# Transposes of keys, queries and outputs moved from TensorE to VectorE by 32-blocks, in a fused DeltaNet and maxout-FFN kernel

## The chip, the cores and the metric

The kernel runs on one core of a Trainium2 chip. The metric is the time on the device in microseconds (us), as the median of a few executions; lower is better. Every run named here was of the undisturbed ("fast") state, and every kernel gave correct results.

The engines are TensorE (PE in the profile, with its weight loads as PEld), VectorE (DVE), ScalarE (ACT), GpSimd (POOL) and SyncE (SP). SyncE only issues transfers. "SPq", "ACTq" and "POOLq" stand for transfers issued by that engine. Each engine works through its own instructions in order: in one run below VectorE stands idle for 43.5 us before six instructions whose data have not landed yet.

## What is computed

A recurrent attention over four batches, eight heads, 768 tokens and a head size of 48, followed by a feed-forward part (FFN) with a maximum over three products:

```python
for t in range(S):                                     # attention, all of (B=4, H=8), D=48
    y[:, :, t] = q_t @ state
    v_old = state.T @ k_t                              # k_t normalised
    state = state + beta_t * outer(k_t, v_t - v_old)
x = y.transpose(0, 2, 1, 3).reshape(B * S, H * D)      # 3072 x 384
h = maximum(maximum(x @ w1, x @ w2), x @ w3)           # 384 -> 768
return h @ w_out                                       # 768 -> 384
```

The kernel cuts the sequence into 12 chunks of 64 tokens. A chunk has two *units* (two batches each), so there are 24 units. Two chunks make a *group* with 512 rows for the FFN. While the FFN of group m runs in 22 pieces, the attention of group m+1 is slipped between its pieces, units of group m+2 are prepared, and data for later ones is loaded.

## The kernel before: the parts that matter

A unit's keys and queries have to be turned before their products (the *gram*, `p_g`) can be made. TensorE does it with eight transposes, and ScalarE copies the result out of PSUM:

```python
def turn(n, parts=(0, 1)):
    kqt = kqts[n]                        # work.tile([128, NP, 2, 2, C], name="kqt", bufs=6)
    p_t = ps_two("p_t")
    for i in parts:                      # keys, queries
        src = (kpad[n % NK], qpad[n % NQ])[i]
        for j in range(NP):              # NP = 4 pairs of heads
            nc.tensor.transpose(p_t[:, i, j * 128 : (j + 1) * 128],
                                src[:, 2 * j : 2 * j + 2], ident)
    ...
    nc.scalar.copy(kqt..., p_t...)
```

A chunk's attention output `y` becomes the input `xt` of the FFN in the same way:

```python
def to_x(c):
    ...
    for g in range(2):
        for t in range(KT):              # KT = 3
            nc.tensor.transpose(p_x[:, g, t * 128 : (t + 1) * 128],
                                y_f[:, g, t * 128 : (t + 1) * 128], ident)
    ...
    copied(c, xt, p_x...)                # ScalarE
```

Which step of the attention comes after which piece of the FFN stands in a table (k, q: products with the state; t: turn; g: gram; z, j, u, s: solve and state; y: output; x: to_x; the digit is the chunk or unit in the group):

```python
LINKS = {
    0: "k0 q0", 1: "t0 t1", 2: "g0 g1", 3: "z0 z1 t2", 5: "j0 j1", 6: "t3",
    7: "u0 g2", 9: "s0 g3", 11: "k1 q1", 13: "u1 y0", 15: "s1", 16: "x0",
    18: "y1", 20: "x1",
}
...
for m in range(1, GROUPS):               # not under manual_schedule
    for i, _ in enumerate(ffn(m)):
        ... loads of k, q, v; solve of group m + 2 from piece 12 on, on VectorE
        links(m + 1, LINKS.get(i, ""))
```

The first part of the kernel keeps its program order by `manual_schedule`. In the loop above there is none, so the order of the instructions on each engine is settled when the kernel is built.

## Time and profile before

| | before |
|---|---|
| time, median of 3 | 612.01 us (610.31 to 614.21) |
| TensorE busy | 560.7 us, 92% |
| VectorE busy | 315.0 us, 52% |
| bytes moved | 45.38 MB |
| from the start of one group's FFN to the next, groups 1 to 4 | 87.4, 87.4, 86.1, 76.5 us |

Three lines of the page of the kernel before: a group of instructions has its line in the kernel's file (L339), engine, operation, output and inputs, shapes, count, then busy time and mean duration in ns, then the idle time just before them. The first line is a queue with packets, megabytes and its share of sixteen DMA engines.

```profile
q1 hardware_dynamic: 132640, 34.01, 29.2%
...
L339 ACT COPY kqt<-p_t 128x512 f32<-128x512 f32 (+1 forms) x32 | 25.0, 796 | 22.2 <-PE p_t L333 22.2
...
L333 PE MATMUL p_t<-ident,kpad 128*128 128x128 f32 x96 | 16.1, 295 | 7.0 <-DVE pt L365 4.7
```

The turning costs TensorE instructions and ScalarE a copy for each unit. What TensorE waited for between 207 and 545 us, that is in groups 1 to 4 (waiting instruction, releaser, total, times, longest):

```profile
PE p_o L721 <- DVE h L707: 2.4, 3, 1.0
PE p_h L697 <- DVE h L707: 0.7, 2, 0.3
```

That is all: 3.1 us in 337.5. The kernel before has almost no slack on TensorE and almost no waits to remove.

### The profile page before, as it was taken

How to read it: one execution, taken by the hardware profiler on the slowest of the kernel's cores; microseconds unless marked ns; L12 is line 12 of the kernel's file. 1: busy time of each engine (PE TensorE's matmuls, PEld its weight loads, DVE VectorE, ACT ScalarE, POOL GpSimd, SP SyncE). 2: the span in 40 equal slices, each digit the busy share in tenths (PEclk: the TensorE clock that was granted, in tenths of full speed). 3: DMA queues.
4: the chain of work that ended last, by engine and by line, in shares of the span. 5: the costliest groups of instructions: out<-in, count | busy, mean ns of one | idle time of the engine just before them, and what ended most of it. 6: DMA issues, size and time to landing. Idle time of an engine off the chain costs nothing.

```text
span 611.2 us, 18549 instructions
## 1 busy us (share of the span) xinstructions
PE 560.7 (92%) x8270; PEld 345.4 (57%) x8270; DVE 315.0 (52%) x730; ACT 155.1 (25%) x284; POOL 70.7 (12%) x102
## 2 busy tenths in 40 slices
PE   5547884998999999999999999999999999999997
PEld 5436774787655565555655545655556545554443
DVE  3454789859369652389532498522696322101110
ACT  4222444643322232221332211331112111110000
POOL 6331544432001000010000000000000000000000
PEclk9755578999999999999999999999999999999999
DMA  9964892942641363321542321522104000010002
GB/s 154 176 168 109 186 194 94 236 96 61 115 67 27 87 117 61 72 54 26 105 85 60 66 48 27 109 54 62 19 15 92 18 2 3 14 40 0 0 1 52
DMA packets 142095, 45.38 MB, mean 74 GB/s; under 512 B 127680, under 2 KB 137728, under 8 KB 142016
## 3 DMA queue, kind: packets, MB, share of 16 engines
q1 hardware_dynamic: 132640, 34.01, 29.2%
q10 hardware_dynamic: 8576, 8.26, 4.8%
q0 software_dynamic: 800, 1.93, 1.2%
q8 instruction: 65, 1.06, 0.7%
q14 instruction: 14, 0.11, 0.1%
HBM read 29.98 MB, written 14.16 MB: 72 GB/s over the span
## 4 chain that ended last, share of the span: by engine, by line
PE 71%; DVE 15%; DMA 6%; issue 3%; SPq 2%; ACT 1%; POOL 1%; POOLq 0%; ACTq 0%; DVEq 0%
PE p_h L697 39%; PE p_o L721 16%; DMA w_bits<-in_moe_w_dram 3%; DVE y_bl L452 3%; DVE tmp L448 3%; PE p_g L355 3%; PE p_t L333 3%; PE p_k L584 2%; PE p_u L612 2%; PE p_y L650 2%; PE p_q L584 1%; DVE h L707 1%; PE p_j L566 1%; PE p_e L515 1%; DVE t L499 1%
## 5 line engine op out<-in xcount | busy, mean ns | idle before, releaser
L697 PE MATMUL p_h<-xt,w_sb 128*128 128x512 f32 (+1 forms) x702 | 297.9, 571 | 1.8 <-DVE xt L683 1.2
L697 PEld LDWEIGHTS p_h<-xt,w_sb 128*128 128x128 f32 x702 | 129.9, 193 | 124.4 <-issue 114.8
L707 DVE TENSOR_TENSOR h<-h,p_h 128x512 f32<-128x512 f32 (+1 forms) x78 | 50.2, 644 | 135.1 <-PE p_h L697 134.9
L721 PE MATMUL p_o<-wo_sb,h 128*128 128x384 f32 x288 | 96.9, 490 | 2.4 <-DVE h L707 2.4
L721 PEld LDWEIGHTS p_o<-wo_sb,h 128*128 128x128 f32 x288 | 53.4, 190 | 40.8 <-DVE h L707 6.8
L452 DVE TENSOR_TENSOR y_bl<-y_bl,tmp 128x31 f32<-128x31 f32 (+20 forms) x154 | 54.0, 351 | 4.1
L448 DVE TENSOR_TENSOR tmp<-x_bl,y_bl 128x31 f32<-128x31 f32 (+20 forms) x154 | 52.8, 343 | 4.2
L705 ACT COPY h<-p_h 128x512 f32<-128x512 f32 (+1 forms) x39 | 21.5, 551 | 119.0 <-PE p_h L697 118.9
L274 POOL TENSOR_TENSOR v_t<-v_t,nrm 128x768 f32<-128x768 f32 x12 | 17.9, 1492 | 275.8 <-DMA v_t<-in_v_dram 179.8
L355 PE MATMUL p_g<-kqt 64*64 64x64 f32 (+1 forms) x1280 | 32.1, 248 | 3.9 <-ACT kqt L339 3.8
L355 PEld LDWEIGHTS p_g<-kqt 64*64 64x64 f32 x1280 | 27.7, 147 | 9.6 <-ACT kqt L339 5.7
L729 ACT COPY o_sb<-p_o 128x384 f32<-128x384 f32 x24 | 11.4, 477 | 79.5 <-PE p_o L721 78.3
L339 ACT COPY kqt<-p_t 128x512 f32<-128x512 f32 (+1 forms) x32 | 25.0, 796 | 22.2 <-PE p_t L333 22.2
L499 DVE STREAM_TRANSPOSE t<-ut 32x256 f32<-32x256 f32 x48 | 20.7, 432 | 6.0 <-DMA ut<-y_d 5.2
L612 PEld LDWEIGHTS p_u<-v_t,ut 64*64 64x64 f32 x768 | 14.4, 148 | 15.6 <-issue 8.5
L612 PE MATMUL p_u<-v_t,ut 64*64 64x48 f32 x768 | 16.1, 234 | 7.3 <-DVE ut L569 4.5
L333 PE MATMUL p_t<-ident,kpad 128*128 128x128 f32 x96 | 16.1, 295 | 7.0 <-DVE pt L365 4.7
L333 PE MATMUL p_t<-ident,qpad 128*128 128x128 f32 x96 | 16.7, 301 | 6.1 <-DMA qpad<-in_q_dram 5.7
L235 POOL TENSOR_TENSOR w_sb<-mant,up 128x384 int32<-128x384 int32 x18 | 18.1, 1005 | 26.9 <-DVE mant L231 18.1
L365 DVE TENSOR_TENSOR pt<-p_g,mask 128x512 f32<-128x512 f32 x24 | 16.5, 690 | 8.7 <-PE p_g L355 8.5
L208 ACT ACTIVATE mant<-w_bits 128x384 f32<-128x384 f32 x24 | 13.3, 556 | 22.3 <-DMA w_bits<-in_moe_w_dram 11.8
L373 ACT COPY at<-p_g 128x512 f32<-128x512 f32 x20 | 11.6, 585 | 29.0 <-DVE pt L365 26.5
(95 smaller groups left out, 489.7 us busy)
## 6 DMA issues: line engine op xcount, KB each, us to landing
w_bits<-in_moe_w_dram ACTq DMA_DIRECT2D x14, 384.0 KB, 4.2
at_d<-at SPq DMA_DIRECT2D x36, 128.0 KB, 2.5
qpad<-in_q_dram SPq DMA_DIRECT2D x48, 96.0 KB, 3.2
v_t<-in_v_dram SPq DMA_DIRECT2D x24, 192.0 KB, 4.0
out_dram<-o_sb SPq DMA_DIRECT2D x48, 96.0 KB, 2.2
kpad<-in_k_dram SPq DMA_DIRECT2D x44, 96.0 KB, 3.9
y_d<-y_bl SPq DMA_DIRECT2D x12, 256.0 KB, 3.3
ut<-y_d SPq DMA_DIRECT2D x48, 64.0 KB, 2.8
```

The lines of the kernel that those rows point to most:

```text
L333: nc.tensor.transpose(p_t[:, i, j * 128 : (j + 1) * 128], src[:, 2 * j : 2 * j + 2], ident,)
L339: nc.scalar.copy(kqt.rearrange("p j b i t -> p i (j b) t")[:, some], p_t.rearrange("p i (x t) -> p i x t", t=C)[:, some],)
L355: nc.tensor.matmul(p_g[rows(bb ^ (g * i)), par, c0 : c0 + C * (1 + whole)], kq[:, 0], kq if whole else kq[:, i],)
L448: nc.vector.tensor_tensor(out=t_v, in0=row.to_broadcast(t_v.shape), in1=column.to_broadcast(t_v.shape), op=ALU.mult,)
L452: nc.vector.tensor_tensor(out=rest, in0=rest, in1=t_v, op=ALU.subtract)
L499: nc.vector.transpose(out=t1[c % NU][block(bb ^ g), g], in_=ut[c % NU][block(bb), g, :, 0:BL])
L584: nc.tensor.matmul(p_b[rows(bb), par, c0 : c0 + D], kqt[g][rows(par), j, bb ^ g, i], st[rows(par), bb ^ g, g, j],)
L612: nc.tensor.matmul(p_v[rows(bb ^ g), g, h], ut[c % NU][rows(bb), g, h], rhs[rows(bb), g, h],)
L697: nc.tensor.matmul(p_h, w_sb[i][:, t, f * 128 : (f + 1) * 128], xt[:, t, lo : lo + w], start=(t == 0), stop=(t == KT - 1),)
L705: nc.scalar.copy(h, p_h)
L707: nc.vector.tensor_tensor(out=h, in0=h, in1=p_h, op=ALU.max)
L721: nc.tensor.matmul(p_o, hs[f][:, i * 128 : (i + 1) * 128], wo_sb[:, f], start=(f == 0), stop=(f == FT - 1),)
```

## The change

The intent is to take the transposes off TensorE. VectorE can turn 32x32 blocks, so the transfers have to put the right blocks in the right partitions.

- Units 12 to 23: `load_blocks` brings keys (on SyncE) and queries (on GpSimd) in 16 transfers a unit, and `turn_blocks` turns them with four VectorE instructions. The tail of each buffer is set to zero by GpSimd.
- Chunks 4 to 11: `y_blocks` writes the output to DRAM in two transfers and reads it back in four, all on SyncE; `turn_y` turns it with one VectorE instruction. The FFN weights are loaded with rows ordered "(p t)" to fit.
- The buffers of both kinds, `turned` and `y_q`, share the four of tag `w_bits`.
- The table of links is rearranged.

```diff
+    def load_blocks(n):
+        c, g = divmod(n, 2)
+        for i in range(2):
+            t = turned[n, i] = work.tile(
+                [128, 2, TURNED], FP32, name="turned", tag="w_bits", bufs=4
+            )
+            nc.gpsimd.memset(t[:, :, TURNED - 48 : TURNED], 0.0)
+            for bb in range(2):
+                for par in range(2):
+                    for db in range(2):
+                        ...
+                        (nc.sync, nc.gpsimd)[i].dma_start(out=t[p0 : p0 + 32, ...], in_=(k, q)[i][...])
+    def turn_blocks(n):
+        kqts[n] = work.tile([128, NP, 2, 2, C], FP32, name="kqt", bufs=6)
+        for i in range(2):
+            t = turned.pop((n, i))
+            for bb in range(2):
+                nc.vector.transpose(out=kqts[n][:, :, bb ^ (n % 2), i]..., in_=t[:, bb, ...])
 ...
+    def y_blocks(c):
+        y = yts.pop(c)
+        y_d = dram.tile([32, 2, 4, DM], FP32, name="y_x")
+        for g in range(2):
+            nc.sync.dma_start(out=y_d[:, g]..., in_=y[:, g]...)
+        y_q = yqs[c] = work.tile([128, 8, 96], FP32, name="y_q", tag="w_bits", bufs=4)
+        for a in range(4):
+            nc.sync.dma_start(out=y_q[32 * a : 32 * (a + 1)], in_=y_d[:, :, :, 96 * a : 96 * (a + 1)]...)
+    def turn_y(c):
+        ...
+        nc.vector.transpose(out=xts[m][:, :, cc * 256 : (cc + 1) * 256]..., in_=yqs.pop(c)...)
 ...
     LINKS = {
-        0: "k0 q0", 1: "t0 t1", 2: "g0 g1", 3: "z0 z1 t2", 5: "j0 j1", 6: "t3",
-        7: "u0 g2", 9: "s0 g3", 11: "k1 q1", 13: "u1 y0", 15: "s1", 16: "x0",
-        18: "y1", 20: "x1",
+        0: "k0 q0", 1: "t0 t1", 2: "g0 g1", 3: "z0 z1", 4: "t2", 5: "j0 j1",
+        6: "u0 t3", 7: "g2", 8: "s0", 9: "g3", 10: "k1 q1", 12: "u1 y0", 13: "x0",
+        14: "s1", 16: "y1", 17: "x1 X0", 21: "X1",
     }
```

(Cut: the access patterns; the same index change in gram and the products with the state; strided reads in `to_x`; the places where loads are issued. In the new table "x" sends a chunk's output to DRAM and back, "X" turns it.)

More of the change, by code (lines that the diff above doesn't have):

```diff
@@ L105, in rows, with dims @@
         return slice(C * bb, C * (bb + 1))
+    def dims(par):
+        return slice(DP * par, DP * par + D)
     def load(src, dst, n, queues):
@@ L172 @@
         for w_t, w in zip(w_sb, (moe_w1, moe_w2, moe_w3)):
-            bits = w.bitcast(U32).rearrange("(t p) f -> p t f", p=128)
+            bits = w.bitcast(U32).rearrange("(p t) f -> p t f", p=128)
             cols = slice(f * 128, (f + 1) * 128)
@@ L342, in turn @@
         )
+    BLOCKS = 12
+    TURNED = 32 + NP * 2 * D + 16
+    turned = {}
+    def load_blocks(n):
[8 more added lines that the diff above has]
+                    for db in range(2):
+                        p0, at = DP * par + 32 * db, 32 * (1 - db)
+                        (nc.sync, nc.gpsimd)[i].dma_start(
+                            out=t[p0 : p0 + 32, bb, at : at + NP * 2 * D].rearrange(
+                                "p (j x) -> p j x", j=NP
+                            ),
+                            in_=(k, q)[i][
+                                2 * bb + g, :, c * C : (c + 1) * C, :
+                            ].rearrange(
+                                "(j two) (r tb) d -> two r j (tb d)", two=2, tb=2
+                            )[par],
+                        )
+    def turn_blocks(n):
[3 more added lines that the diff above has]
+            for bb in range(2):
+                nc.vector.transpose(
+                    out=kqts[n][:, :, bb ^ (n % 2), i].rearrange(
+                        "p j (r tb) -> p j tb r", tb=2
+                    ),
+                    in_=t[:, bb, 32 : 32 + NP * 2 * D].rearrange(
+                        "p (j tb d) -> p j tb d", tb=2, d=D
+                    )[:, :, :, 0:32],
+                )
     def gram(n, parts=(0, 1), queues=one_queue, copy=nc.scalar.copy):
@@ L351, in gram @@
                 for bb in range(2):
-                    kq = kqt[rows(par), j, bb ^ g]
+                    kq = kqt[dims(par), j, bb ^ g]
                     for i in (0,) if whole else parts:
@@ L585, in times_state @@
                             p_b[rows(bb), par, c0 : c0 + D],
-                            kqt[g][rows(par), j, bb ^ g, i],
-                            st[rows(par), bb ^ g, g, j],
+                            kqt[g][dims(par), j, bb ^ g, i],
+                            st[dims(par), bb ^ g, g, j],
                         )
@@ L668, in to_x @@
                     p_x[:, g, t * 128 : (t + 1) * 128],
-                    y_f[:, g, t * 128 : (t + 1) * 128],
+                    y_f[:, g, t::KT],
                     ident,
@@ L675, in to_x @@
         copied(c, xt, p_x[:, :, 0 : KT * 128].rearrange("p g (t x) -> p g t x", t=KT))
+    yqs = {}
+    def y_blocks(c):
+        y = yts.pop(c)
+        y_d = dram.tile([32, 2, 4, DM], FP32, name="y_x")
+        for g in range(2):
+            nc.sync.dma_start(
+                out=y_d[:, g].rearrange("t b x -> b t x"),
+                in_=y[:, g].rearrange("p h d -> p (h d)"),
+            )
+        y_q = yqs[c] = work.tile([128, 8, 96], FP32, name="y_q", tag="w_bits", bufs=4)
+        for a in range(4):
+            nc.sync.dma_start(
+                out=y_q[32 * a : 32 * (a + 1)],
+                in_=y_d[:, :, :, 96 * a : 96 * (a + 1)].rearrange(
+                    "t g b x -> t (g b) x"
+                ),
+            )
+    def turn_y(c):
+        m, cc = divmod(c, 2)
+        if m not in xts:
+            xts[m] = work.tile([128, KT, TOK], FP32, name="xt")
+        nc.vector.transpose(
+            out=xts[m][:, :, cc * 256 : (cc + 1) * 256].rearrange(
+                "p t (b x) -> p b t x", x=32
+            ),
+            in_=yqs.pop(c).rearrange("p b (x t) -> p b t x", t=KT),
+        )
     def copied(c, to, of):
@@ L850, in links @@
             f, i = name[0], int(name[1])
-            if f in BY_CHUNK and m < GROUPS:
+            if f in "xX" and 2 <= m:
+                if m < GROUPS:
+                    (y_blocks if f == "x" else turn_y)(2 * m + i)
+            elif f in BY_CHUNK and m < GROUPS:
                 BY_CHUNK[f](2 * m + i)
@@ L857, in links @@
             elif f in BY_UNIT and m + 1 < GROUPS:
-                BY_UNIT[f](4 * (m + 1) + i)
+                n = 4 * (m + 1) + i
+                (turn_blocks if f == "t" and n >= BLOCKS else BY_UNIT[f])(n)
     by_hand = ExitStack()
@@ L891 @@
             load_k(i - 15)
-            if i < 30:
-                load_q(i - 15)
+            if i < 29:
+                load_blocks(i - 15)
     some(solving, 40)
@@ L901 @@
                 load_k(n)
-                if n % 4 < 3:
-                    load_q(n)
+                if i < 20:
+                    load_blocks(n)
             if m + 2 < GROUPS:
                 n0 = 4 * (m + 2)
-                if i == 2:
-                    load_q(n0 + 3)
+                if i in (1, 3):
+                    load_blocks(n0 + 2 + i // 3)
                 if i in (6, 9):
```

## The prediction

> **What bounds the kernel now.** I read the page's first two parts, then the busy time by stage, the chain that ended last in order of time, the timelines of each engine in one stage, and who waited for whom.
>
> The page of the kernel before, busy time, slices and the chain by line:
> ```profile
> PE 560.7 (92%) x8270; PEld 345.4 (57%) x8270; DVE 315.0 (52%) x730; ACT 155.1 (25%) x284; POOL 70.7 (12%) x102
> ...
> PE   5547884998999999999999999999999999999997
> ...
> DVE  3454789859369652389532498522696322101110
> ```
> PE is at 9 tenths from about slice 9 on; VectorE comes next, and unevenly. The mean hides stages, so I cut the span where the feed-forward (FFN) of each group of four units begins. The busy time of each engine in five such stretches:
> ```profile
> 207.27:294.70 87.43, 86.06 (x1290) 49.49 (x1289) 51.46 (x124) 21.68 (x36) 3.04 (x2) 1.00 0.34 67
> 294.70:382.14 87.44, 86.04 (x1290) 49.46 (x1289) 50.77 (x120) 21.63 (x36) 2.95 (x2) 1.00 0.34 68
> 382.14:468.28 86.14, 85.83 (x1289) 49.61 (x1289) 46.77 (x106) 19.08 (x30) 1.47 (x1) 1.00 0.25 52
> 468.28:544.80 76.52, 76.52 (x1002) 41.63 (x1001) 19.00 (x29) 12.51 (x20) 0.00 (x0) 1.00 0.11 24
> 544.80:611.00 66.20, 61.83 (x156) 29.34 (x155) 8.25 (x12) 5.90 (x11) 0.00 (x0) 0.99 0.07 15
> ```
> The columns are length, busy time of PE, weight loads, VectorE, ScalarE and GpSimd, clock, DMA share, GB/s. In groups 1 to 4 PE is busy 98.4 to 100% of the time at full clock: what is taken off PE there shortens the kernel, until something else has to be waited for. The last stretch, with FFN alone, takes 61.8 us of PE time; the other 15 to 26 us of a group are the next group's attention, and the transposes are in those. The chain in order of time (start, length, what), one group's pieces of it:
> ```profile
> 302.06 1.75 PE p_t L333 x16
> ...
> 312.52 1.02 PE p_t L333 x8
> ...
> 322.71 0.87 PE p_t L333 x8
> ...
> 377.61 0.66 PE p_x L667 x6
> ```
> The chain runs through the transposes, so they are paid for in full.
>
> **What the Trainium skill says.** "VectorE: DVE Perf Modes", section "The three transpose paths": TensorE turns a whole 128x128 tile into PSUM, VectorE turns 32x32 blocks separately, SBUF to SBUF. That is why the change must have the right 32-blocks placed by DMA first. The trace times both kinds: 128x512 stream transposes take 690 ns and 32x256 ones 432 ns, so about 1.0 ns an element of a row plus 0.17 us, and a TensorE transpose in a row costs 1.75/16 = 0.109 us of the chain, though a single one is shown as 295 to 301 ns. "DMA: Bandwidth & Descriptors", section "Anatomy of one DMA": a transfer has a fixed cost of about 2 us, mostly the receipt. The trace agrees: 2.0 us for a 2 KB transfer, 2.2 to 4.0 us for the ordinary ones. "SBUF — State Buffer", section "Who interferes with whom": a VectorE instruction with two SBUF inputs blocks against a GpSimd instruction that reads SBUF, one with a single input outside the two-port modes does not. The trace agrees: an update of y_bl with 112 columns took 1.43 us instead of 0.28 while the scaling of v_t ran on GpSimd. The new block transposes have one input, so this should not touch them.
>
> **The change part by part.**
>
> *Off PE.* Units 12 to 23 are turned during groups 1 to 3, four in each. A unit has 8 transposes; a group 1.75 + 1.02 + 0.87 = 3.64 us, three groups 10.9 us. Chunks 4 to 11 are turned in groups 1 to 4, two in each, 6 transposes in 0.65 us: 8 x 0.65 = 5.2 us. Together 16.1 us, all on the chain. That is the most the intended saving can be: 612.0 - 16.1 = 595.9 us, or 2.6%. ScalarE also loses 12 copies of 1.0 us and 8 of 0.8 us, and the bank pairs in PSUM are less in demand; ScalarE was not the bound, so this is worth nothing by itself.
>
> *Onto VectorE.* A unit needs 4 block transposes of 128x256, each like the 256-element row above, 0.43 us: 1.7 us, 12 units 20.7 us. A chunk's output is one of 128x768: 0.17 + 768 x 1.0 ns = 0.95 us, 8 chunks 7.6 us. So 28 us, 8.8 us in a group that had 51 of 87 us: 60 of about 82, 73%. That fits in the mean. It isn't even, though: the block solve runs in the last third of a group, and there (256.0 to 294.7) VectorE is busy 31.8 of 38.7 us, from 263.7 on almost without a gap. The two output transposes fall right there.
>
> *Onto the queues.* A unit no longer loads q in two transfers with 192-byte rows, but has 16 transfers of 128 rows of 384 B, 8 for k on SyncE and 8 for q on GpSimd. k is still loaded untransposed as well. On the SyncE queue a transfer occupies about 0.55 us (8 loads of ut: 4.15 to 5.44 us). A group adds 32 and takes away 8, and the outputs add 2 x 6: 36 x 0.55 = 20 us more beside some 54 x 0.57 = 31 us, within 82 us. GpSimd gets 32 x 0.55 = 18 us, where it had 3. Bytes: 8 x 128 x 2 x 384 B = 0.79 MB a unit less 0.20 MB of q, so +2.4 MB a group, and the outputs out and back 2 x 0.79 = 1.6 MB: 5.9 to about 9.8 MB. At the 21.5 ns a packet of 256 B that queue 1 shows (29.2% of 16 x 611 us over 132,640 packets), so perhaps 30 ns at 384 B, that is 10 to 14 us of all sixteen engines' time more, share 0.34 to about 0.5. The transfers stay hidden in bulk.
>
> *New waits.* The output of a group's second chunk now takes a path through DRAM before the next group can begin: addition 0.95, write issue and landing 0.6 + 3.0, four reads 2.2 + 3.0, transpose 0.95, and hand-overs, about 12 us. Between the last y (after piece 16) and the next group PE has one FFN piece of 2.58 us and four of 3.87: 18 us. So it fits by 6 us, if neither the SyncE queue, in order, nor VectorE is held up. The blocks, y_q and the w_bits share four buffers; the second unit of the next group gets its buffers only when the two outputs have been turned.
>
> *The rearranged links.* Attention steps move up one or two pieces, filling the places of the transposes. A small effect of either sign: PE's idle time in groups 1 and 2 is only 1.4 us each.
>
> *The solve.* The gram of a group's last unit stays at piece 9 and starts the solve, so the solve begins about 3.6 us earlier in the group while the group is 5 us shorter. With 1.9 us of output transposes in its way it ends about 1.5 us after the next group begins (before: 293.8 against 294.7), and y_d and ut take some 9 to 12 us more (before: ut landed near 302). p_z, now about 14 us into the group, had 9 us of room and keeps 1 to 4.
>
> *Elsewhere.* Chunks 0 to 3 are transposed from rows with a stride of three: 24 weight loads, under 1 us if at all. Contracting over 48 instead of 64 rows doesn't change the columns streamed, so I count nothing.
>
> *Sum.* -16.1 us, plus 0 to 2 us at each of four group boundaries (output path), 0 to 2 us at three (solve and ut), and 0.3 to 0.5 us per group for maxima that come late behind block transposes: around 4 us given back. 612.0 - 16.1 + 4 = 600, and with the rearranged links, made to fill exactly these holes, I say 599.
>
> **The rivals.** (1) VectorE takes the bound in the last third of each group: the maxima of h queue behind solve and output transposes. For it: the only PE waits in groups 1 and 2 are already there, for h. Against it: one transpose is under 1 us, an FFN piece lasts 2.58 us and has two PSUM buffers. It would give back 2 to 3 us a group, for 604 to 608. (2) The path through DRAM or the late ut becomes the wait at group boundaries. For it: margins of 6 and of 1 to 4 us and a SyncE queue with two thirds more to issue. Against it: that queue idles half of a group now. At 3 us a boundary: 606 to 609. (3) Everything hides: 595 to 596. (4) VectorE's in-order queue waits for blocks that land later than planned, and PE for kqt: several us a group, 612 or more; I hold this unlikely, as the loads run three pieces (8 us) ahead and landings took 2.5 to 4 us.
>
> **Range and chances.** The limit below is the full saving, 595.9, less about 1 us for luck with the links; above, rival 2 or 1 nearly whole. 595 to 608 us, predicted 599. The threshold of 2% is 599.8, that is three quarters of the full saving, so the chances are nearly even: faster by over 2% 0.52, within 2% 0.43, slower by over 2% 0.05.
>
> **What would show it.** No p_t or p_x in groups 1 to 4, and those stretches 4 to 5 us shorter (the fourth 1.3); PE still 97% busy or more there. 48 stream transposes near 0.43 us and 8 near 0.95. If PE waits for xt at a group's start, the DRAM path failed; if for ut or z, the solve did; if for h, VectorE's queue; if for kqt, the loads. I'd be wrong below 595 if the new links remove waits that I took for PE work, and above 608 if block transposes take far longer than 0.43 us with a strided output or the SyncE queue stands behind a buffer wait.

## The result

The changed kernel took **655.79 us** in the median (654.04 to 658.15, four runs) against 611.84 us of the kernel before in the same rounds. The ratio is 1.072 (95% interval 1.067 to 1.077): slower by 7%. A ratio here is always the mean time of one kernel's fast runs over the mean of the other's in the same rounds, so it is not quite the quotient of the medians. The prediction was wrong, and its range did not hold the time.

The page of the changed kernel, first busy times, then two rows of 40 slices: TensorE's busy share, and PEclk, the clock that it was granted, both in tenths:

```profile
PE 568.7 (87%) x8126; PEld 338.3 (52%) x8126; DVE 342.9 (52%) x786; ACT 134.6 (21%) x264; POOL 126.6 (19%) x222
...
PE   6556977899999999989889976897993699999997
...
PEclk9755587999999999999899996898897799999999
```

There are 144 fewer instructions on TensorE, as meant, yet it is busy 8 us longer, and there are holes in the slices with a lower clock in and after them. The same stretches as before, cut at the start of each group's FFN (length, then busy time of TensorE, weight loads, VectorE, ScalarE and GpSimd, clock, DMA share, GB/s):

```profile
206.80:294.20 87.40, 82.28 (x1246) 44.76 (x1244) 58.25 (x141) 15.19 (x30) 9.23 (x15) 1.00 0.42 90
294.20:398.90 104.70, 89.68 (x1372) 48.78 (x1373) 56.16 (x127) 14.83 (x28) 20.02 (x42) 0.93 0.41 93
398.90:514.20 115.30, 92.61 (x1245) 49.00 (x1245) 58.32 (x138) 15.10 (x30) 16.78 (x31) 0.87 0.34 76
514.20:589.90 75.70, 75.59 (x861) 39.33 (x862) 21.50 (x35) 9.66 (x16) 0.00 (x0) 0.98 0.19 44
```

Everything is in two stretches. The four sum to 383.1 us against 337.5 before, 45.6 more, as much as the whole. Group 2 is 17.3 us longer, group 3 29.2 us. Groups 1 and 3 have nearly the same TensorE instructions, 1246 and 1245 with the same count of each product to within one, but in group 3 TensorE idles 22.7 us instead of 5.1 and is busy 10.3 us longer at a clock of 0.87. So of the 27.9 us between those two, 17.6 are idle and 10.3 go with the lowered clock. What TensorE waited for in the changed kernel from 200 to 545 us:

```profile
PE p_h L776 <- DVE tmp L495: 15.5, 1, 15.5
PE p_h L776 <- DVE xt L749: 12.4, 2, 9.7
PE p_h L776 <- ACT h L784: 7.6, 4, 1.9
PE p_g L402 <- DVE kqt L382: 1.9, 2, 1.5
```

The two great waits are those of the first `p_h` of a group, the consumer of `xt`. In order of time on TensorE, these are the starts of groups 2, 3 and 4 (start, length, instructions, wait in brackets):

```profile
294.18 2.81 PE L776 MATMUL p_h<-xt,w_sb 128*128 128x512 f32 x6 [2.71 <-DVE xt L749]
...
398.92 5.46 PE L776 MATMUL p_h<-xt,w_sb 128*128 128x512 f32 x6 [9.70 <-DVE xt L749]
...
514.19 12.18 PE L776 MATMUL p_h<-xt,w_sb 128*128 128x512 f32 x24 [15.46 <-DVE tmp L495]
```

The last one is named after `tmp`, an instruction of the solve. But VectorE's transpose into `xt` ran from 512.86 to 514.05, just ahead of it, and was the last input that `p_h` needed; the 15.5 us, too, are a wait for `xt`. And after the 9.70 us of idle time six `p_h` took 5.46 us, nearly twice the 2.81 us that they took after 2.71 us.

**Why is `xt` late?** Three views show it for the end of group 2. First SyncE's own list:

```profile
372.91 1.14 SPq L732 DMA_DIRECT2D y_x<-y  x2
376.15 4.34 SPq L811 DMA_DIRECT2D out_dram<-o_sb  x3
380.90 2.54 SPq L738 DMA_DIRECT2D y_q<-y_x  x4
383.49 3.92 SPq L366 DMA_DIRECT2D turned<-in_k_dram  x8
...
389.51 4.28 SPq L366 DMA_DIRECT2D turned<-in_k_dram  x8
```

The second chunk's output goes out at 372.9. Its reading back has to wait until that has landed, stands behind three result transfers, which wait for the FFN's last products, and is issued 8 us later. The keys of two later units stand behind that. Then GpSimd at the same time:

```profile
373.82 4.35 POOL L366 DMA_DIRECT2D turned<-in_q_dram  x8
385.29 0.18 POOL L361 MEMSET turned<- 128x96 f32 x1 [7.13 <-DVE xt L749]
398.84 0.18 POOL L361 MEMSET turned<- 128x96 f32 x1 [13.37 <-DVE xt L749]
```

The memory of the next unit's blocks is that of `y_q`, so the clearing of the new buffer waits 7.1 and 13.4 us for the output transposes, and the queries' transfers wait behind the clearing. Third, the grams. Before, in that group, the last two units' were at 327.06 and 334.38, that is 32.5 and 39.8 us after the group began. The last one before, then those of the changed kernel:

```profile
334.38 1.19 PE L355 MATMUL p_g<-kqt 64*64 64x64 f32 x64
...
339.98 1.10 PE L402 MATMUL p_g<-kqt 48*64 48x128 f32 x30 [0.40 <-DVE kqt L382]
...
349.17 0.27 PE L402 MATMUL p_g<-kqt 48*64 48x64 f32 x2
...
352.45 1.02 PE L402 MATMUL p_g<-kqt 48*64 48x64 f32 x53
```

The bulk of the last gram starts 58 us into the group, 18 us later than before, and it is scattered in pieces over TensorE's order. Its blocks were not late: the last of them were issued by 320.4, but VectorE turned the last two only at 348.16 and 351.37, without a wait for them; from 207 to 515 us it waited only 6.0 us for blocks in all. Here the built order is late, not the load. The solve needs all four units, so VectorE starts it late; and the second `xt` stands behind the solve in VectorE's order. The blocks of that chunk were issued by 383.4, but turned at 397.59.

What SyncE's queue waited for (total, times, longest), from 207 to 515 us, first before and then in the changed kernel:

```profile
SPq L381 <- ACT at L373: 15.4, 5, 6.2
...
SPq L428 <- ACT h L784: 67.2, 4, 22.6
SPq L738 <- DMA y_x<-y: 15.4, 7, 5.5
```

L381 and L428 are the same transfer, `at_d<-at`: it takes a copy of the gram, made by ScalarE, to the solve. With its smaller entries it held the head of the queue for 80.9 us, against 15.9 before. So a late gram also delays the outputs and the key blocks that stand behind this transfer: lateness feeds itself through the queue.

This much the trace says. It does not say which link of the loop is the cause: loads late, buffers held, the built order, or the way through DRAM by itself. That is for the runs.

### The profile page after: what moved, and what is told of

It is laid out like the page before. It is cut to its first block, busy times and chain, and to the rows that moved or that the text cites. A ratio compares the mean times of both kernels' runs of the same rounds, so it can differ in the third digit from the quotient of the medians.

```text
span 656.4 us, 18744 instructions
## 1 busy us (share of the span) xinstructions
PE 568.7 (87%) x8126; PEld 338.3 (52%) x8126; DVE 342.9 (52%) x786; ACT 134.6 (21%) x264; POOL 126.6 (19%) x222
## 3 DMA queue, kind: packets, MB, share of 16 engines
q8 instruction: 64, 1.05, 0.7%
## 4 chain that ended last, share of the span: by engine, by line
PE 58%; DVE 22%; DMA 11%; issue 5%; ACT 2%; POOL 1%; SPq 1%; DVEq 0%; POOLq 0%; ACTq 0%
PE p_h L776 38%; DVE y_bl L499 6%; DVE tmp L495 6%; PE p_o L800 6%; DMA w_bits<-in_moe_w_dram 3%; PE p_g L402 3%; DMA kpad<-in_k_dram 2%; PE p_u L659 2%; DMA y_d<-y_bl 2%; PE p_s L680 1%; PE p_y L697 1%; DMA ut<-y_d 1%; DVE t L546 1%; DVE pt L412 1%; DMA x_bl<-at_d 1%
## 5 line engine op out<-in xcount | busy, mean ns | idle before, releaser
L776 PE MATMUL p_h<-xt,w_sb 128*128 128x512 f32 (+1 forms) x702 | 315.6, 597 | 38.0 <-DVE tmp L495 15.5
L776 PEld LDWEIGHTS p_h<-xt,w_sb 128*128 128x128 f32 x702 | 133.9, 200 | 167.7 <-issue 147.7
L800 PE MATMUL p_o<-wo_sb,h 128*128 128x384 f32 x288 | 94.7, 487 | 1.2 <-DVE h L786 1.2
L366 POOL DMA_DIRECT2D turned<-in_q_dram x96 | 52.2, 551 | 2.5 <-issue 2.0
L402 PE MATMUL p_g<-kqt 48*64 48x64 f32 (+1 forms) x1280 | 36.3, 251 | 5.6 <-ACT kqt L342 3.7
L402 PEld LDWEIGHTS p_g<-kqt 48*64 48x64 f32 x1280 | 29.3, 149 | 22.9 <-issue 14.0
L659 PE MATMUL p_u<-v_t,ut 64*64 64x48 f32 x768 | 18.2, 235 | 6.6 <-DVE ut L616 4.5
L659 PEld LDWEIGHTS p_u<-v_t,ut 64*64 64x64 f32 x768 | 15.8, 149 | 15.0 <-issue 8.6
L382 DVE STREAM_TRANSPOSE kqt<-turned 128x256 f32<-128x256 f32 x48 | 18.5, 422 | 6.1 <-DMA turned<-in_k_dram 3.6
L215 POOL TENSOR_SCALAR mant<-mant 128x384 f32<-128x384 f32 x24 | 12.9, 538 | 22.2 <-ACT mant L211 21.0
```

Source lines behind the costliest of these rows:

```text
L366: (nc.sync, nc.gpsimd)[i].dma_start(out=t[p0 : p0 + 32, bb, at : at + NP * 2 * D].rearrange("p (j x) -> p j x", j=NP), in_=(k, q)[i][2 * b ...
L382: nc.vector.transpose(out=kqts[n][:, :, bb ^ (n % 2), i].rearrange("p j (r tb) -> p j tb r", tb=2), in_=t[:, bb, 32 : 32 + NP * 2 * D].rea ...
L402: nc.tensor.matmul(p_g[rows(bb ^ (g * i)), par, c0 : c0 + C * (1 + whole)], kq[:, 0], kq if whole else kq[:, i],)
L659: nc.tensor.matmul(p_v[rows(bb ^ g), g, h], ut[c % NU][rows(bb), g, h], rhs[rows(bb), g, h],)
L776: nc.tensor.matmul(p_h, w_sb[i][:, t, f * 128 : (f + 1) * 128], xt[:, t, lo : lo + w], start=(t == 0), stop=(t == KT - 1),)
L800: nc.tensor.matmul(p_o, hs[f][:, i * 128 : (i + 1) * 128], wo_sb[:, f], start=(f == 0), stop=(f == FT - 1),)
```

## The experiments

Eighteen kernels were run. All outputs are right. "Before" is always the kernel before in the same rounds; its medians lay between 611.19 and 612.30 us.

### One part alone

**Only the new table of links**, on the kernel before:

```diff
-        7: "u0 g2", 9: "s0 g3", 11: "k1 q1", 13: "u1 y0", 15: "s1", 16: "x0",   # and the rest of the old table
+        6: "u0 t3", 7: "g2", 8: "s0", 9: "g3", 10: "k1 q1", 12: "u1 y0", 13: "x0",   # and the rest of the new one
```

> The kernel before with nothing but the new table of links (the X entries do nothing). If the rearrangement of the attention steps did harm by itself: over 620 us. All theories that blame blocks or outputs: 612 us within 1% (606 to 618).

Measured: 619.67 us, ratio 1.013 (1.008 to 1.017). With its TensorE transposes left in, the new table costs 7.4 us: `x0` and `x1` come one piece after `y0` and `y1`, where there were three and two, and `p_x` waits 5.1 us for `y`. So the table is not neutral. Whether it suits a kernel without those transposes was not run: outputs of both chunks through DRAM with the old table are missing.

**Only keys and queries in blocks**, with the old table and outputs on TensorE:

```diff
-            if f in "xX" and 2 <= m:
-                if m < GROUPS:
-                    (y_blocks if f == "x" else turn_y)(2 * m + i)
-            elif f in BY_CHUNK and m < GROUPS:
+            if f in BY_CHUNK and m < GROUPS:
     LINKS = { ...old table... }
```

> Outputs on PE again and the table of links of the kernel before; only keys and queries in blocks. The run with the new links (606.9 us) left PE waiting 4.3 us for y and h in front of p_x. If those waits come from the new links: they go, and 601 to 604 us, near 612.3 - 10.9 = 601.4. If from VectorE's block transposes: 605 to 608 us as before.

Measured: **603.37 us** (601.68 to 606.19), ratio 0.986 (0.982 to 0.990). This half does what was predicted of it. Two of its stretches, to be laid beside those of the kernel before:

```profile
208.00:291.80 83.80, 82.72 (x1257) 46.31 (x1256) 55.99 (x141) 17.04 (x32) 21.68 (x42) 1.00 0.49 97
291.80:374.90 83.10, 82.85 (x1258) 46.32 (x1257) 54.99 (x137) 17.30 (x32) 21.72 (x42) 1.00 0.48 99
```

TensorE has 3.3 and 3.2 us less work in these groups and idles no more than before. VectorE at 55 to 56 of 83 us is no bound, and a DMA share of 0.48 to 0.49 does no harm.

**The same, with the old order of the weights' rows**, so that TensorE reads unstrided rows of `y`:

```diff
-            bits = w.bitcast(U32).rearrange("(p t) f -> p t f", p=128)
+            bits = w.bitcast(U32).rearrange("(t p) f -> p t f", p=128)
...
-                    y_f[:, g, t::KT],
+                    y_f[:, g, t * 128 : (t + 1) * 128],
```

> Keys and queries in blocks alone on the kernel before: outputs on PE, old links, and also the old order of the weights' rows, so that PE's transposes of outputs read unstrided rows. The measured 603.4 us of the same with strided rows minus what the stride costs: 602 to 603.5 if the strided weight loads cost 0 to 1.5 us, as they are 147 to 199 ns each; the same 603.4 if they don't matter.

Measured: **602.82 us** (600.46 to 605.24), ratio 0.985 (0.982 to 0.989). A strided weight load of `p_x` takes a median of 195 ns, an unstrided one 142, but the times of the two kernels cannot be told apart. This is the lowest median found, 9 us below the kernel before and 53 below the changed one.

**Keys and queries in blocks with the new table**, outputs on TensorE: the same edit as in the second run, without the old table.

> The changed kernel with the outputs of all chunks transposed by PE again; keys and queries stay in blocks. Theory A (the next group waits for xt because its transpose stands behind the solve in VectorE's order): the waits of PE for xt (12 + 15 us) go, and the kernel comes near 612 - 10.9 + 4 = 605 us, 600 to 612. Theory B (the block loads come late, so the grams and the solve are late): groups 2 and 3 stay near 100 us, 640 us or more.

Measured: 606.86 us, ratio 0.992 (0.988 to 0.996). The new table takes back 3.5 us of the gain.

**Only outputs through DRAM, with the new table**, keys and queries on TensorE:

```diff
-    BLOCKS = 12
+    BLOCKS = 24
...
-            if i < 29:
-                load_blocks(i - 15)
+            if i < 30:
+                load_q(i - 15)          # and likewise in the groups
```

> The changed kernel with keys and queries of all units transposed by PE again; only the outputs go through DRAM and VectorE. Theory A alone: PE still waits for xt at the starts of groups 2 to 4, over 5 us each, 625 us or more. Theory B (the late solve comes from the late blocks, and only a late solve makes xt late): the solve starts about 56 us into the group again, waits for xt are under 3 us a group, 605 to 615 us.

Measured: 615.63 us, ratio 1.009 (1.003 to 1.014), with two waits of 2.5 us for `xt`. By the medians that is 4.0 us less than the new table alone, near the 5.2 us of `p_x` that were taken off; but the intervals of the two ratios overlap, so the gain is not shown.

With the new table in all four:

| | outputs on TensorE | outputs through DRAM |
|---|---|---|
| keys, queries on TensorE | 619.7 | 615.6 |
| keys, queries in blocks | 606.9 | 655.8 |

Keys and queries give 12.8 us and outputs 4.0 (within noise). If these added up, the changed kernel would take 602.8 us. **53 us come only when both parts are there.** Neither part does harm of this size by itself; it lies in what they share or disturb in each other.

### Is it the way of the outputs by itself?

**The same work without the dependency:** TensorE makes `xt`, and the outputs still go through DRAM and VectorE, but into a tile that nobody reads (the solve's scratch tile has one buffer instead of two, and `y` is kept longer):

```diff
-                    (y_blocks if f == "x" else turn_y)(2 * m + i)
+                    if f == "x":
+                        to_x(2 * m + i, y_blocks(2 * m + i))
+                    else:
+                        turn_y(2 * m + i)
...
-            out=xts[m][:, :, cc * 256 : (cc + 1) * 256]...
+            out=spare...
```

> The changed kernel, but PE makes xt as before, and the outputs' whole way (out to DRAM, back, VectorE's transpose) is done as well, into a tile that nobody reads; results right. If the harm is the wait of the next group for xt (dependency): 605 to 617 us, little more than the run with outputs on PE. If it is the work itself on VectorE, on the queues and in the four shared buffers: 640 us or more, without any PE wait for xt.

Measured: 641.31 us, ratio 1.048 (1.046 to 1.050). Nobody waits for the outputs' way any more, the wait that the trace showed so large is gone, and still 29 of the 44 us remain; TensorE now waits for ScalarE's and VectorE's work on `h` (11.8 and 5.1 us). Of the 29, 5.2 us are the `p_x` that are back. So, by difference, the dependency on `xt` is worth up to some 20 us, and the other 24 come with the mere presence of these transfers, transposes and buffers, and with the order built for them.

**Only the first chunk of each group through DRAM**, then **only the second**:

```diff
-                if m < GROUPS:
+                if m < GROUPS and i == 1:        # second run: i == 0
+                    if f == "x":
+                        to_x(2 * m + i)
+                elif m < GROUPS:
                     (y_blocks if f == "x" else turn_y)(2 * m + i)
```

> The changed kernel with only the first chunk of each group going through DRAM and VectorE; the second is transposed by PE. The first chunk's xt is ready long before the next group. If the harm is the wait at the boundary: 603 to 612 us. If the buffers or the queues do it, half of the traffic is left: 615 to 640 us.

> The reverse: only the second chunk of each group goes through DRAM and VectorE. If the wait at the boundary is the harm: nearly all of the 44 us stays, 640 us or more. If buffers or queues: 615 to 640 us, much like the first chunk alone.

Measured: 622.10 us, ratio 1.016 (1.011 to 1.021), and 634.45 us, ratio 1.036 (1.033 to 1.040). In the table the first chunk is turned four pieces before the end of a group, and TensorE waited only 2.4 us for `xt` in all (5.5 in the second run). Still the first chunk costs 15 us over the 606.86 of the version with neither. The second costs 28, and both together 49, a little more than the sum. This again speaks against a single tight path at the end of a group, and for something that each output takes from the rest; what it takes, these two runs do not show.

### Is it the built order?

**TensorE in program order in groups 1 to 5:**

```diff
+    by_hand = ExitStack()
+    by_hand.enter_context(tc.manual_schedule(engines={mybir.EngineType.PE}))
     for m in range(1, GROUPS):
...
         some(solving, 40)
+    by_hand.close()
```

> The changed kernel with PE's instructions in program order in groups 1 to 5 as well (the grams had been moved behind FFN pieces in groups 2 and 3). If the moved grams are the cause of the late solve: the gram of the last unit back at about 36 us into the group, and 625 us or less. If the data are late anyway (block loads, xt): PE waits for kqt instead, and 650 us or more.

Measured: 626.69 us, ratio 1.025 (1.021 to 1.028). That gives back 29 us. Three waits for `xt` remain, 13.5 us, the longest 7.2. The last gram of group 2 is back in one piece, 42 us into the group, and TensorE waits only 3.0 us for `kqt` in all. The order that was built for TensorE is an important part of the loss.

**TensorE and VectorE in program order:** the same with `{PE, DVE}`.

> The changed kernel with both PE and VectorE in program order in groups 1 to 5. If the order fixed at compile time (transposes set late among the solve's steps and grams set late on PE) is what makes the data arrive late: better than PE alone in program order (626.7 us), 605 to 620 us. If the data themselves land late: VectorE in order stalls on them, and 627 us or more.

Measured: 676.19 us, ratio 1.105 (1.102 to 1.108), the slowest of all; waits for `xt` rose to 40.3 us in three. Held to program order, VectorE stands before data that has not come yet, 43.5 us before `ut` alone. So program order is no cure for VectorE: its built order avoids some of these waits.

**The outputs with high priority in the built order:**

```diff
-                    (y_blocks if f == "x" else turn_y)(2 * m + i)
+                    with tc.high_priority():
+                        (y_blocks if f == "x" else turn_y)(2 * m + i)
```

> The changed kernel with the outputs' way through DRAM and their transposes at high priority for the scheduler, which in groups 2 and 3 puts both transposes ahead of the solve on VectorE. Theory A: PE's waits for xt fall under 3 us a group, but the solve now ends later, so p_z may wait; 640 us or less. Theory B: the buffers come free earlier too, so it also predicts a gain, but no more than own buffers give. If neither: 650 us or more.

Measured: 654.94 us, ratio 1.069 (1.066 to 1.073). The output transposes of groups 2 and 3 did move ahead of the solve: in this trace the second one of group 2 runs at 384.25, before the solve and 10 us ahead of the next group, and TensorE's waits for `xt` fell from the 12.4 and 15.5 us to 2.8 (groups 3 and 4 began with waits of 3.1 and 3.9 us named after ScalarE's `o_sb`). But the time did not change. VectorE now idles 17.2 us at two of these transposes, until their data has landed, the solve comes later still, and TensorE waits for `kqt` (9.6 us), `h` (8.3 us) and others. That `xt` stands behind the solve was plain in the trace of the changed kernel, but it isn't the cause.

### Is it the queue or the buffers?

**Own buffers for the outputs**; to make room, the solve's scratch tile keeps one buffer of two:

```diff
-        y_q = yqs[c] = work.tile([128, 8, 96], FP32, name="y_q", tag="w_bits", bufs=4)
+        y_q = yqs[c] = work.tile([128, 8, 96], FP32, name="y_q", tag="mant", bufs=2)
...
-            tmp = work.tile([128, 256], FP32, name="tmp")
+            tmp = work.tile([128, 256], FP32, name="tmp", bufs=1)
```

> The changed kernel with two buffers of its own for the returning outputs (in the place of a scratch tile of the weight conversion; the solve's scratch tile has one buffer instead of two to make room). Theory A (xt stands behind the solve in VectorE's fixed order, whatever the buffers): within 3% of the changed kernel, 636 us or more, PE still waits over 8 us for xt. Theory B (outputs and blocks share four buffers, so the next group's second unit can only be loaded when the last output is turned, and each group is late for the next): the grams return to their places, 630 us or less.

Measured: 649.87 us, ratio 1.061 (1.057 to 1.066). 6 us of 44. What the smaller scratch tile costs by itself was not run; it is part of every run with own buffers below.

**Program order on TensorE, own buffers and priority together:** the three edits above.

> The changed kernel with PE in program order, own buffers for the outputs and their priority, all three. If order and buffers are the whole cause: 603 to 615 us, little waiting for xt. If a cost remains that none of them touches (VectorE's time, the queues): over 620 us.

Measured: 632.29 us, ratio 1.032 (1.028 to 1.037): 5.6 us worse than the order alone. So with SyncE's queue left as it was, neither order, buffers nor priority led below 626 us.

**The key blocks on ScalarE's queue instead of SyncE's**, buffers shared:

```diff
-                        (nc.sync, nc.gpsimd)[i].dma_start(
+                        (nc.scalar, nc.gpsimd)[i].dma_start(
```

> The changed kernel with the k blocks issued on ScalarE's queue instead of SyncE's; buffers shared as before. If the in-order SyncE queue (loads standing behind the outputs' transfers) makes the loads late and through them grams, turns and solve, 620 to 635 us. If the shared buffers hold the loads back, whichever queue they stand on, 645 to 660. If the compile-time order alone is at fault, no more than 10 us either way, unless the order changes by itself.

Measured: 626.33 us, ratio 1.025 (1.022 to 1.028). 29 us come back by changing only who issues 96 transfers. No wait for `xt` is left among TensorE's; the largest are two for `kqt`, 8.3 us together, and GpSimd still waits 45.8 us for `xt` before it clears buffers.

**The outputs' transfers on ScalarE's queue**, buffers shared:

```diff
-            nc.sync.dma_start(
+            nc.scalar.dma_start(
                 out=y_d[:, g]...                  # and the four reads likewise
```

> The changed kernel with the outputs' transfers on ScalarE's queue and the buffers still shared: the fourth corner beside the changed kernel (655.8), own buffers alone (649.9) and both (608.9). If SyncE's in-order queue is what matters and the buffers are not, 608 to 616 us. If each of the two holds the loads back by itself, so that removing one leaves the other, 635 to 655.

Measured: 620.57 us, ratio 1.015 (1.011 to 1.019).

**The same with own buffers for the outputs:**

> The changed kernel with both of the outputs' transfers on ScalarE's queue and with two buffers of their own for the outputs, so loads of blocks meet the outputs neither in SyncE's queue nor in the buffers. If contention of loads and outputs explains the interaction of 44 us, 615 to 630 us; if the fixed orders on PE and VectorE do by themselves, 640 to 655.

Measured: **608.93 us** (608.56 to 610.56), ratio 0.996 (0.994 to 0.998). 47 us come back, with every TensorE transpose of the change gone, the new table in place and the built order free. The four corners:

| | buffers shared | own buffers for outputs |
|---|---|---|
| outputs on SyncE's queue | 655.8 | 649.9 |
| outputs on ScalarE's queue | 620.6 | 608.9 |

The queue gives 35 to 41 us, the buffers 6 to 12. The 620.6 us lie outside both bands of the expectation. Shared buffers do not hold the loads back by themselves, since moving the queue alone removes 35 us; the shared queue keeps nearly all of the loss by itself, since own buffers alone remove only 6. The stretches of this kernel:

```profile
208.20:299.20 91.00, 86.21 (x1380) 47.83 (x1379) 60.61 (x151) 16.08 (x31) 26.56 (x53) 0.98 0.55 117
299.20:383.40 84.20, 82.07 (x1241) 44.91 (x1240) 54.49 (x132) 15.55 (x30) 16.80 (x31) 1.00 0.51 108
383.40:466.70 83.30, 82.24 (x1243) 44.94 (x1242) 52.43 (x126) 13.89 (x26) 2.95 (x2) 1.00 0.37 79
466.70:541.00 74.30, 73.70 (x862) 38.49 (x861) 20.37 (x30) 10.01 (x17) 0.00 (x0) 1.00 0.19 44
```

Groups 2 to 4 are 3.2, 2.8 and 2.2 us shorter than before, at full clock. Group 1 is 3.6 us longer than before. It does 134 TensorE instructions more than in the changed kernel (stretch 4 has 862, where the kernel with program order below has 989, so work has moved one group ahead), and its longest wait is 2.1 us. The grams of group 2 on TensorE, and the second chunk's output on VectorE:

```profile
326.56 1.10 PE L402 MATMUL p_g<-kqt 48*64 48x128 f32 x32
...
334.22 1.22 PE L402 MATMUL p_g<-kqt 48*64 48x64 f32 x64
...
379.18 1.22 DVE L749 STREAM_TRANSPOSE xt<-y_q 128x768 f32<-128x768 f32 x1
```

The last gram starts 35.0 us into the group (58 in the changed kernel, 39.8 before) and in one piece, and `xt` is ready 3 us before it is needed at 383.4. What GpSimd's clearing of block buffers waits for has changed as well: it was `xt`, 45.2 us in all, and now it is mainly the turning of older blocks, as meant:

```profile
POOL turned L361 <- DVE kqt L382: 63.7, 11, 11.9
```

**The same, with TensorE in program order:**

> The same as the kernel with outputs on ScalarE's queue and own buffers, and PE kept in program order in groups 1 to 5. If the two causes (contention for queue and buffers, and PE's order) add up, 605 to 615 us, as 626.7 were left with PE's order alone. If the path of the second output through VectorE's place behind the solve is what remains, 622 to 630 as before.

Measured: 612.64 us, ratio 1.002 (0.998 to 1.007). With TensorE's order fixed and the same, moving the outputs and giving them buffers is worth 14 us (626.7 to 612.6). With the order free it is worth 47. The program order, which helped by 29 us while the queue was shared, now costs 4. So about 14 us of the loss are lateness that shows under a fixed order. The other 33 came only together with the free order, which looks quite different in the two traces: scattered, late grams in one, whole and early ones in the other. Moving transfers has moved the order of an engine that issues none of them; by what rule it was built, and which of its rearrangements costs how much, was not separated.

### Can the outputs' half gain at all?

**Keys and queries in blocks with the old table, and only the first chunk's output through DRAM**, on ScalarE's queue with own buffers:

```diff
     LINKS = { ...old table...
-        18: "y1", 20: "x1",
+        18: "y1", 20: "x1 X0",
     }                                  # plus i == 1 back on TensorE, own buffers, ScalarE's queue, as above
```

> Keys and queries in blocks, old links, and only the first chunk's output of each group through DRAM on ScalarE's queue with buffers of its own; PE turns the second. From the 603.4 us of blocks alone four transposes of six (0.65 us each, 2.6 us) go off PE. If contention and lateness of the second chunk were the whole trouble, 600 to 602 us; if the outputs' path costs something by itself even with time to spare, 603 to 608.

Measured: 607.28 us (606.64 to 608.39), ratio 0.993 (0.989 to 0.996): 4 us slower than keys and queries alone, although four times 0.65 us went off TensorE. TensorE's largest wait from 205 to 540 us, and one of ScalarE's:

```profile
PE p_h L776 <- ACT h L784: 7.3, 4, 2.5
```

```profile
ACT h L784 <- DMA y_x<-y: 19.2, 3, 6.7
```

The reads back wait for the write to land, and on ScalarE's queue they stand in front of ScalarE's own copies of `h`, for which TensorE waits. In the kernel with keys and queries alone TensorE's waits were 1.8 us altogether. So here, too, the cost is work that stands behind a wait, now on ScalarE. Whether the outputs would gain on a queue that has neither loads nor copies behind it stays open. The nearest to it is the fourth corner above, with its outputs turned by VectorE and yet 6 us behind keys and queries alone (2 us behind them with the same new table).

## Why the prediction was wrong

**Right.** The transposes of keys and queries were on the path: 8.9 us net of the predicted 10.9. No `p_t` or `p_x` is left in groups 1 to 4 of the changed kernel. VectorE does not become the bound (rival 1), and its transposes from blocks cost what was said. The DMA share rose to 0.42 in the first group (0.49 with keys and queries alone, 0.55 with the outputs on ScalarE's queue and own buffers), for about 0.5 forecast, and was harmless in bulk: the runs with more of it are the faster ones. The two lines of the changed kernel's VectorE:

```profile
L382 DVE STREAM_TRANSPOSE kqt<-turned 128x256 f32<-128x256 f32 x48 | 18.5, 422 | 6.1 <-DMA turned<-in_k_dram 3.6 <-DMA turned<-in_q_dram 2.4
L749 DVE STREAM_TRANSPOSE xt<-y_q 128x768 f32<-128x768 f32 x8 | 9.6, 1205 | 7.7 <-DMA y_q<-y_x 7.7
```

422 ns for 430 predicted; 1205 ns for 950, a miss of 2 us of VectorE's time over the kernel. Contracting over 48 rows instead of 64 changed nothing: a product of the gram took 246 ns with keys and queries alone, 248 before. (The section on one DMA that the prediction cites is about transfers that GpSimd issues; the 2.0 us that the prediction sets beside it are those of SyncE's 2 KB transfers.)

**The step that failed** is *New waits*: "So it fits by 6 us, if neither the SyncE queue, in order, nor VectorE is held up." The condition was named and then taken as met. The room was right: at the end of group 2 TensorE still had 17.3 us of work after the second `y` (371.94 to 389.22), for 18 forecast. The path was wrong: from that `y` to the finished `xt` at 398.78 it took 26.8 us instead of about 12, and TensorE stood still for 9.7 us. The reads were issued 6.9 us after the writes, behind the result transfers, and the transpose began 14.2 us after the last read was issued, behind the solve.

SyncE's queue was counted as occupied time (51 of 82 us) and found with room. But a queue in order is not filled by the time of its transfers alone; it stands still for the longest wait of whatever is at its head. In the changed kernel the reads of `y_q` waited 15.4 us in seven instances for the write of `y_x` to land, `at_d` 80.9 us for its copy of late grams, and result transfers for `p_o`, with outputs and the keys of later units behind them. Moving the 48 output transfers off that queue gave back 35 us, and with own buffers 47, most of it together with another order on TensorE. The prediction's own sign for a time above 608 us, a SyncE queue that "stands behind a buffer wait", came true in kind: SyncE stood behind data, and GpSimd behind buffers (45.2 us).

The next sentence of that step, on blocks and outputs sharing four buffers, named a second part of the loss without giving it a size; measured 6 to 12 us.

**Rivals.** Rival 2 named the right place, but its size, 3 us a boundary, came from margins in a timetable that the lateness itself moves: measured 2.7, 9.7 and 15.5 us. Rival 4 held that loads would be late and several us a group be lost, and was called unlikely since "the loads run three pieces (8 us) ahead". On SyncE's queue they do stand behind the outputs, but TensorE waited only 1.9 us for `kqt`, VectorE only 6.0 us for blocks, and the last blocks of group 2 were issued 28 us before they were turned: what came late there was their place in the built order. Both rivals held a part of the loss, and 53 us of it come only with both parts of the change.

**What no step contained.** The loss is more than its waits. In group 3, 10.3 of the 27.9 us over group 1 go with TensorE's slower clock; the Trainium skill tells of this in "TensorE: Matmul & The Clock Gate", section "Part 1: The HAM clock gate (the "warmup" mystery)", where an idle window of about 3.4 us halves the clock. The wait of 9.70 us agrees: six `p_h` after it took 5.46 us, at a granted clock of 0.50, and 2.81 us after a wait of 2.71. But no such threshold comes out of these traces: with only the first chunk through DRAM, six `p_h` took 5.46 us, again at 0.50, after a wait of 2.39. And the order in which TensorE does its work was not a constant: in the changed kernel it set the last gram 18 us later. Program order on TensorE gave back 29 us.

**The rearranged links** were said to be "a small effect of either sign". Alone they cost 7.4 us, with keys and queries in blocks 3.5, and so they took about 40% of the real gain.

**Open.** How the 33 us that go through the built order divide among its rearrangements, and whether the outputs' half can gain on an undisturbed queue. At best, its 5.2 us of `p_x` are at stake. The query blocks stayed on GpSimd's queue in every run; what a move of them would do is not known.

## What to carry to other kernels

For each transfer you add to an in-order queue, ask what it waits for and what stands behind it, not only how long it takes; a store that waits for a result, and a reload that waits for the store, do not belong on the queue, or in the buffers, of prefetches. Take a change apart before you judge it: here one half gains 9 us, the other, with its new table, loses 3, and both together lose 44. When the order of instructions is built for you, a moved transfer can reorder engines that it never touches, so compare the orders of the two traces, and test with the order fixed.

## What the Trainium skill lacked or had wrong

- "DMA: Bandwidth & Descriptors", section "Issuing engines are not separate DMA queues", says that issuing from several engines only saves the issue time on the sequencer, which is usually small. Here the issuing engine of 48 transfers was worth 35 us (655.8 to 620.6 us with buffers shared), in part through the order that was built for TensorE: with that order fixed, queue and buffers together were worth 14. The same page's section on the anatomy of one DMA says that a semaphore's wait is spent on the issuing sequencer before dispatch; it does not draw the consequence that everything behind that transfer waits as well. Here: 15.4 us of SyncE's time in waits of `y_q` reads for `y_x`, and 19.2 us of waits of ScalarE's `h` copies behind them in the run that put the first chunk's outputs on ScalarE's queue.
- "VectorE: DVE Perf Modes", section "The three transpose paths", has one figure for VectorE, for 128x128 in bf16. For fp32 block transposes the runs show 422 ns for 128x256, 690 for 128x512, and 1205 for 128x768 with a stride of three in its input. From 256 to 512 elements that is 1.05 ns for each further element of a row, and at this rate 768 would take some 960 ns; so the remaining 250 or so go with the stride, an estimate that no run isolated. No page has a figure for such a stride.
- No page read for this case has a figure for a strided weight load of fp32 on TensorE: 195 ns with a stride of three against 142 ns without (`p_x`), which did not show in the time (603.4 and 602.8 us).
